# One of the sums of a Strassen-like product: a GpSimd addition, or a second activation and an adding transfer

## The chip, the cores and the metric

The kernel runs on one core of a Trainium2 chip. The metric is the device time of one execution in microseconds (us), lower is better. The kernel before took 1920.28 us (median of two runs, 1920.08 and 1920.47).

A core has engines that each work through their own instructions in order and wait for one another only through semaphores: TensorE (PE) multiplies matrices and leaves its results in PSUM, VectorE (DVE) and ScalarE (ACT) do elementwise work, GpSimd (POOL) does elementwise work on SBUF, and SyncE (SP) issues transfers here. Transfers run on 16 DMA engines; GpSimd, too, can issue them.

## The reference

Two parts, one behind the other. The first is the real part of a two-dimensional Fourier transform of each of 8 batches of 3008 x 256 numbers. The second is a small network on the 24064 rows that result: 256 to 2048 columns, the quick GELU, and back to 256.

```python
def _attn_ref(x):                       # x: (8, 3008, 256)
    X = np.fft.fft(x, axis=1)
    X = np.fft.fft(X, axis=2)
    return X.real.astype(np.float32)

def _moe_ref(x, w_in, w_out):           # x: (24064, 256)
    h = x @ w_in                        # w_in: (256, 2048)
    g = h * (1.0 / (1.0 + np.exp(-1.702 * h)))
    return (g @ w_out).astype(np.float32)
```

## The kernel before

All data are float32. The work is cut into steps: 8 batches, each with 3 blocks of 2 halves, each half with 8 pieces p of 256 hidden columns, so 384 steps in all. One step takes up to 256 columns of the transform (225 in one of the six halves).

In step t the kernel makes the hidden layer of step t and, with a lag of three steps, the product with w_out of step t-3. The hidden values of a step are four blocks of 128 partitions x n columns: h[:, half, f], with half for two mirrored frequencies and f for two groups of 128 hidden columns. They are called a11, a12, a21 and a22.

For the first 8 steps the product is done in the ordinary way. From step 8 on (t >= NP) it uses seven multiplications for a 2 x 2 block product in place of eight, in the manner of Strassen and Winograd. That needs four sums of the activated blocks for each step:

- s1 = a21 + a22 and s3 = a11 - a21, made by GpSimd;
- s2 = s1 - a11 and s4 = a12 - s2, made by VectorE.

```python
def hidden(t):                                   # TensorE, then ScalarE
    ...
    pa, pb = bank("pa"), bank("pb")              # PSUM, four banks in turn: two steps
    for ps, cs in ((pa, 0), (pb, 1)):
        for i in range(2):
            f = 2 * p + i
            nc.tensor.matmul(ps[:, i * 256:i * 256 + n], lhsT=wcs[cs][:, f * 128:(f + 1) * 128],
                             rhs=pq[:, cs, ks], start=True, stop=True)
    v = sp.tile([128, 512], F32, tag="v", name="v")
    nc.scalar.copy(two(v[:], n), two(pa[:], n))
    vb[t] = v, pa, pb

def rows(t):                                     # VectorE: the four blocks before the activation
    ...
    h = ht[t] = hp.tile([128, 2, 2, 256], F32, tag="h", name="h")     # four buffers
    dif = sp.tile([128, 512], F32, tag="dif", name="dif")
    nc.vector.tensor_tensor(two(h[:], n), two(v[:], n), two(pb[:], n), op=ALU.add)
    for i in range(2):
        ...
        nc.vector.scalar_tensor_tensor(dif[...], nb[:, ks], af2[:, f:f + 1], pb[...], op0=ALU.mult, op1=ALU.subtract)
    ...
            nc.vector.tensor_tensor(<second half of h, mirrored in runs of 32>, pa, dif, op=ALU.add)

def activate(t):                                 # ScalarE, in place
    b, blk, hh, p = steps[t]
    g = free(ht[t][:], 0, [256, 4], [1, width(blk, hh)])
    nc.scalar.activation(g, g, ACTF.Gelu_apprx_sigmoid)

def sums(t, eng):
    if not NP <= t < len(steps):
        return
    h, n = ht[t], width(*steps[t][1:3])
    a11, a12, a21, a22 = h[:, 0, 0, :n], h[:, 0, 1, :n], h[:, 1, 0, :n], h[:, 1, 1, :n]
    if eng is nc.gpsimd:
        st[t] = sp.tile([128, 4, 256], F32, tag="s", bufs=3, name="s")
    s1, s2, s3, s4 = (st[t][:, q, :n] for q in range(4))
    if eng is nc.gpsimd:
        eng.tensor_tensor(s1, a21, a22, op=ALU.add)
        eng.tensor_tensor(s3, a11, a21, op=ALU.subtract)
    else:
        eng.tensor_tensor(s2, s1, a11, op=ALU.subtract)
        eng.tensor_tensor(s4, a12, s2, op=ALU.subtract)

def product(t):                                  # TensorE, 14 matmuls; (bank, half, weights, data, ...)
    ...
        plan = ((0, 0, wo[:, p, 0, :], h[:, 0, 0, :n], 0), (0, 1, wt[:, p, 1, :], s[:, 1, :n], 0),
                (1, 0, wo[:, p, 2, :], h[:, 0, 1, :n], 0), (1, 1, wt[:, p, 2, :], s[:, 2, :n], 0),
                (2, 0, wt[:, p, 0, :], s[:, 0, :n], 0), (2, 1, wo[:, p, 3, :], s[:, 3, :n], 0),
                (3, 0, wt[:, p, 3, :], h[:, 1, 1, :n], 0))
    ...
```

The page counts each float32 matmul as two records, so the 4 matmuls of the hidden layer and the 7 of the product stand there as 8 and 14.

The order of a step in the program is the order in which each engine gets its work:

```python
for t in range(n + LAG):                         # LAG = 3
    if t < n:
        hidden(t)
    ...
    if t >= LAG:
        product(t - LAG)
    ...
    if 0 < t <= n:
        activate(t - 1)
        sums(t - 1, nc.gpsimd)
    sums(t - 2, nc.vector)
    if t < n:
        rows(t)
    if t >= LAG:
        combine(t - LAG)                         # VectorE, once in 8 steps: 7 operations, 2 transposes, stores
    for fn, args in extra.get(t, ()):            # the transform of the next batch, among the steps:
        fn(*args)                                # folds of x on GpSimd, small products, loads by SyncE
```

At the end there is no next step: the products of the last two steps are merged behind the third to last.

Of the kernel before, what the change touches and what calls it, by code (L numbers as in the profile page):

```python
# [27 lines left out]
F32 = mybir.dt.float32  # L28
U32 = mybir.dt.uint32
ALU = mybir.AluOpType  # L30
ACTF = mybir.ActivationFunctionType
# [15 lines left out]
def view(ap, offset, *dims):  # L47
    return bass.AP(ap.tensor, ap.offset + offset, [list(d) for d in dims])


def free(ap, offset, *dims):
    return bass.AP(ap.tensor, ap.offset + offset, [list(ap.ap[0])] + [list(d) for d in dims])
# [59 lines left out]
def kernel(ctx: ExitStack, tc, x, w_in, w_out, tab1, tab2, out):  # L112
    nc = tc.nc
# [12 lines left out]
    sp = ctx.enter_context(tc.tile_pool(name="sp", bufs=2, space=SB))  # L126
    op = ctx.enter_context(tc.tile_pool(name="op", bufs=2, space=SB))
# [330 lines left out]
    NP = NF // 2  # L458
    steps = [(b, blk, hh, p) for b in range(B) for blk in range(NBLK) for hh in range(2) for p in range(NP)]
    vb, ht, st, pot, ot = {}, {}, {}, {}, {}  # L460

    def width(blk, hh):

        return 225 if (blk, hh) == (0, 1) else 256
# [38 lines left out]

    def activate(t):
        b, blk, hh, p = steps[t]
        g = free(ht[t][:], 0, [256, 4], [1, width(blk, hh)])
        nc.scalar.activation(g, g, ACTF.Gelu_apprx_sigmoid)  # L507

    def sums(t, eng):

        if not NP <= t < len(steps):
            return
        h, n = ht[t], width(*steps[t][1:3])
        a11, a12, a21, a22 = h[:, 0, 0, :n], h[:, 0, 1, :n], h[:, 1, 0, :n], h[:, 1, 1, :n]
        if eng is nc.gpsimd:
            st[t] = sp.tile([128, 4, 256], F32, tag="s", bufs=3, name="s")
        s1, s2, s3, s4 = (st[t][:, q, :n] for q in range(4))
        if eng is nc.gpsimd:
            eng.tensor_tensor(s1, a21, a22, op=ALU.add)  # L519
            eng.tensor_tensor(s3, a11, a21, op=ALU.subtract)  # L520
        else:
            eng.tensor_tensor(s2, s1, a11, op=ALU.subtract)  # L522
            eng.tensor_tensor(s4, a12, s2, op=ALU.subtract)  # L523
# [115 lines left out]
    for e in odds:  # L639
# [7 lines left out]
                      in_=view(tab1, 0, [tab1.shape[1], 128], [28 * NM, 2], [1, ends]))  # L647
# [73 lines left out]
    n = len(steps)  # L721
# [38 lines left out]
    for t in range(n + LAG):  # L760
        if t < n:
            hidden(t)
        if t == 0:
            low_up(in2)
            nyquist(0, 0)
            low_down(in2)
        if t in rows_at:
            first_row(rows_at[t])
        if t >= LAG:
            product(t - LAG)  # L770
        if t in early:
            fold_w(early[t])
# [8 lines that stand above are left out]
            combine(t - LAG)  # L781
        for fn, args in extra.get(t, ()):
            fn(*args)
# [28 lines left out]
```

## Time and profile before

| | busy, us | share of the span | instructions |
|---|---|---|---|
| TensorE, matmuls | 1907.5 | 99% | 10720 |
| VectorE | 1415.3 | 74% | 2937 |
| GpSimd | 764.2 | 40% | 1057 |
| ScalarE | 675.0 | 35% | 932 |

| operation per step | line | engine | mean, ns | times |
|---|---|---|---|---|
| s1 = a21 + a22 | L519 | GpSimd | 720 | 376 |
| s3 = a11 - a21 | L520 | GpSimd | 735 | 376 |
| s2 = s1 - a11 | L522 | VectorE | 478 | 376 |
| s4 = a12 - s2 | L523 | VectorE | 528 | 376 |
| copy v <- pa | L482 | ScalarE | 578 | 384 |
| activation, in place | L507 | ScalarE | 1044 | 384 |

A row of the groups by line reads: line, engine, operation, what is written and what is read, the shape and the count; then the busy time in us and the mean in ns; then the engine's idle time just before these instructions and what ended most of it. The timeline gives the start in us from the span's start, the duration, the engine, the line, the operation and the count; in brackets stands the idle time before and its releaser. "PEld" is the loading of weights into TensorE, which runs beside the matmuls. The time in which an engine issues a transfer is not counted as busy.

The DMA queues moved 103.54 MB, nearly all from SyncE's queue; there is no transfer from GpSimd's queue.

### The profile page before, as it was taken

What the parts mean: (1) busy time and instruction counts of PE and PEld (TensorE: products, weight loads), DVE (VectorE), ACT (ScalarE), POOL (GpSimd) and SP (SyncE); (2) the same over time, 40 slices, a digit from 0 to 9 for tenths busy, and PEclk for the clock granted to TensorE, in tenths of its full rate; (3) what the DMA queues carried; (4) which work ended last, traced back from release to release, by engine and by line L of the source; (5) the groups of instructions that cost most, each with busy time, mean ns of one, the idle gap of its engine ahead of it and who ended that gap; (6) DMA issues with size and microseconds to landing.
All of it is one profiled execution on the core that took longest, in us unless ns stands there. A gap on an engine that the chain in (4) does not pass through costs nothing.

```text
span 1920.2 us, 29354 instructions
## 1 busy us (share of the span) xinstructions
PE 1907.5 (99%) x10720; PEld 1673.7 (87%) x10720; DVE 1415.3 (74%) x2937; ACT 675.0 (35%) x932; POOL 764.2 (40%) x1057
## 2 busy tenths in 40 slices
PE   8999999999999999999999999999999999999998
PEld 6798888988889888988889888898888988889887
DVE  7777677877787677777777777677777877778766
ACT  6533333333333333333333333333333333333332
POOL 4474224533256223552235523264323542223222
PEclk9999999999999999999999999999999999999999
DMA  8721530335212542226222172121820223202201
GB/s 269 174 51 35 113 36 12 59 57 102 17 23 48 90 69 24 51 28 105 40 28 50 43 107 32 16 49 43 124 19 12 17 50 54 17 12 27 17 12 23
DMA packets 145312, 103.54 MB, mean 54 GB/s; under 512 B 104914, under 2 KB 127986, under 8 KB 143984
## 3 DMA queue, kind: packets, MB, share of 16 engines
q1 hardware_dynamic: 143952, 101.14, 31.4%
q8 instruction: 85, 1.39, 0.3%
q10 hardware_dynamic: 1216, 0.52, 0.1%
q14 instruction: 59, 0.48, 0.1%
HBM read 58.38 MB, written 48.01 MB: 55 GB/s over the span
## 4 chain that ended last, share of the span: by engine, by line
PE 98%; DMA 1%; ACT 1%; DVE 0%; POOL 0%; SPq 0%; issue 0%; ACTq 0%; POOLq 0%
PE po L551 59%; PE pa L478 17%; PE pb L478 17%; PE ps L226 2%; PE ps L328 1%; PE ps L279 1%; DMA wo<-in_tab_dram 0%; DMA raw<-in_moe_w_out_dram 0%; PE psw L444 0%; ACT wo L251 0%; POOL wst L420 0%; PE psf L454 0%; ACT g L374 0%; ACT h L507 0%; DVE m L406 0%; DVE a L408 0%
## 5 line engine op out<-in xcount | busy, mean ns | idle before, releaser
L551 PE MATMUL po<-s,wo 128*128 128x256 f32 (+1 forms) x3008 | 758.4, 375 | 0.0
L519 POOL TENSOR_TENSOR s<-h 128x256 f32<-128x256 f32 (+1 forms) x376 | 270.8, 720 | 1085.0 <-ACT h L507 1020.6
L551 PE MATMUL po<-h,wo 128*128 128x256 f32 (+1 forms) x2384 | 689.3, 375 | 0.0
L551 PEld LDWEIGHTS po<-s,wo 128*128 128x128 f32 x3008 | 571.5, 190 | 64.5
L482 ACT COPY v<-pa 128x512 f32<-128x512 f32 (+1 forms) x384 | 222.1, 578 | 1061.9 <-PE pa L478 1061.9
L492 DVE TENSOR_TENSOR h<-v,pb 128x512 f32<-128x512 f32 (+1 forms) x384 | 259.0, 675 | 400.0 <-PE pb L478 386.6
L551 PEld LDWEIGHTS po<-h,wo 128*128 128x128 f32 x2384 | 452.8, 190 | 51.6
L507 ACT ACTIVATE h<-h 128x1024 f32<-128x1024 f32 (+1 forms) x384 | 400.9, 1044 | 17.9 <-DVE h L502 15.6
L478 PE MATMUL pa<-pq,wcs 128*128 128x256 f32 (+1 forms) x1536 | 393.9, 379 | 1.9 <-ACT h L507 1.7
L478 PE MATMUL pb<-pq,wcs 128*128 128x256 f32 (+1 forms) x1536 | 387.6, 375 | 0.0
L478 PEld LDWEIGHTS pa<-pq,wcs 128*128 128x128 f32 x1536 | 286.7, 190 | 50.5 <-issue 10.2
L495 DVE SCALAR_TENSOR_TENSOR dif<-nb,af,pb 128x256 f32<-128x256 f32 (+1 forms) x768 | 328.4, 469 | 0.9 <-ACT nb L346 0.9
L478 PEld LDWEIGHTS pb<-pq,wcs 128*128 128x128 f32 x1536 | 291.7, 190 | 33.2
L520 POOL TENSOR_TENSOR s<-h 128x256 f32<-128x256 f32 (+1 forms) x376 | 276.5, 735 | 0.0
L502 DVE TENSOR_TENSOR h<-pa,dif 128x512 f32<-128x512 f32 (+1 forms) x448 | 265.5, 605 | 13.2
L523 DVE TENSOR_TENSOR s<-h,s 128x256 f32<-128x256 f32 (+1 forms) x376 | 198.6, 528 | 12.9
L522 DVE TENSOR_TENSOR s<-s,h 128x256 f32<-128x256 f32 (+1 forms) x376 | 179.6, 478 | 4.3 <-POOL s L519 4.3
L199 POOL TENSOR_TENSOR xt<-xt 111x510 f32<-111x510 f32 x56 | 73.5, 1313 | 4.4
L585 DVE TENSOR_TENSOR c<-u,po 128x256 f32<-128x256 f32 (+1 forms) x188 | 69.5, 410 | 2.5 <-PE po L551 0.9
L334 DVE STREAM_TRANSPOSE pq<-ps 128x256 f32<-128x256 f32 x96 | 34.6, 418 | 44.9 <-PE ps L328 44.9
L585 DVE TENSOR_TENSOR u<-u,po 128x256 f32<-128x256 f32 (+1 forms) x141 | 57.8, 410 | 8.2 <-ACT u L556 2.5
L568 DVE STREAM_TRANSPOSE os<-c 128x512 f32<-128x512 f32 x93 | 60.4, 687 | 0.0
(73 smaller groups left out, 512.0 us busy)
## 6 DMA issues: line engine op xcount, KB each, us to landing
out_dram<-os SPq DMA_DIRECT2D x284, 64.0 KB
Td<-xt SPq DMA_DIRECT2D x14, 768.0 KB
t<-Td SPq DMA_DIRECT2D x7, 1536.0 KB
xt<-in_x_dram SPq DMA_DIRECT2D x14, 512.0 KB
xt<-Xr SPq DMA_DIRECT2D x14, 512.0 KB
nb<-pq SPq DMA_DIRECT2D x23, 256.0 KB
out_dram<-os SPq DMA_DIRECT2D x96, 56.0 KB
Xr<-in_x_dram SPq DMA_DIRECT2D x7, 752.0 KB
```

What stands on the lines that cost most here:

```text
L478: nc.tensor.matmul(ps[:, i * 256:i * 256 + n], lhsT=wcs[cs][:, f * 128:(f + 1) * 128], rhs=pq[:, cs, ks], start=True, stop=True)
L482: nc.scalar.copy(two(v[:], n), two(pa[:], n))
L492: nc.vector.tensor_tensor(two(h[:], n), two(v[:], n), two(pb[:], n), op=ALU.add)
L495: nc.vector.scalar_tensor_tensor(dif[:, i * 256:i * 256 + n], nb[:, ks], af2[:, f:f + 1], pb[:, i * 256:i * 256 + n], op0=ALU.mult, op1=AL ...
L502: nc.vector.tensor_tensor(free(h[:], 512 + at + m - 1, [256, 2], [RUN, blocks], [-1, m]), *ins, op=ALU.add)
L507: nc.scalar.activation(g, g, ACTF.Gelu_apprx_sigmoid)
L519: eng.tensor_tensor(s1, a21, a22, op=ALU.add)
L520: eng.tensor_tensor(s3, a11, a21, op=ALU.subtract)
L522: eng.tensor_tensor(s2, s1, a11, op=ALU.subtract)
L523: eng.tensor_tensor(s4, a12, s2, op=ALU.subtract)
L551: nc.tensor.matmul(pot[q][:, i, :n], lhsT=lhs, rhs=rhs, start=(p == 0 and i == 0 and f == 0), stop=(p == NP - 1), skip_group_check=True)
L585: nc.vector.tensor_tensor(out_, i0, i1, op=how)
```

## The change

The sum s1 = a21 + a22 is made in another way. ScalarE activates the raw block a22 a second time, straight into s1, before the in-place activation of all four blocks. Then a transfer from SBUF to SBUF, issued from GpSimd's queue, adds the activated a21 to it. GpSimd's addition of s1 falls away; s3 stays with GpSimd, s2 and s4 stay with VectorE. What is computed is the same. It is meant to take elementwise work off GpSimd, which shares the step with folds of the next batch's x, and give it to ScalarE and the DMA engines, which have more idle time. The buffer for the sums is taken one function earlier; there are still three of them.

```diff
     def activate(t):
         b, blk, hh, p = steps[t]
-        g = free(ht[t][:], 0, [256, 4], [1, width(blk, hh)])
+        n = width(blk, hh)
+        if t >= NP:
+            st[t] = sp.tile([128, 4, 256], F32, tag="s", bufs=3, name="s")
+            nc.scalar.activation(st[t][:, 0, :n], ht[t][:, 1, 1, :n], ACTF.Gelu_apprx_sigmoid)
+        g = free(ht[t][:], 0, [256, 4], [1, n])
         nc.scalar.activation(g, g, ACTF.Gelu_apprx_sigmoid)

     def sums(t, eng):
...
         a11, a12, a21, a22 = h[:, 0, 0, :n], h[:, 0, 1, :n], h[:, 1, 0, :n], h[:, 1, 1, :n]
-        if eng is nc.gpsimd:
-            st[t] = sp.tile([128, 4, 256], F32, tag="s", bufs=3, name="s")
         s1, s2, s3, s4 = (st[t][:, q, :n] for q in range(4))
         if eng is nc.gpsimd:
-            eng.tensor_tensor(s1, a21, a22, op=ALU.add)
+            eng.dma_start(out=s1, in_=a21, accum_op=ALU.add)
             eng.tensor_tensor(s3, a11, a21, op=ALU.subtract)
```

Lines of the changed kernel stand two to four lower than before: VectorE's s2 moves from L522 to L524, s4 from L523 to L525, and the in-place activation from L507 to L511.

## The prediction

> **What bounds the kernel now.** I read the page's first part (busy time of each engine), then the chain that ended last, then the groups by line, and last the timeline of two ordinary steps near the middle.
>
> ```profile
> PE 1907.5 (99%) x10720; PEld 1673.7 (87%) x10720; DVE 1415.3 (74%) x2937; ACT 675.0 (35%) x932; POOL 764.2 (40%) x1057
> PE 98%; DMA 1%; ACT 1%; DVE 0%; POOL 0%; SPq 0%; issue 0%; ACTq 0%; POOLq 0%
> L519 POOL TENSOR_TENSOR s<-h 128x256 f32<-128x256 f32 (+1 forms) x376 | 270.8, 720 | 1085.0 <-ACT h L507 1020.6
> L522 DVE TENSOR_TENSOR s<-s,h 128x256 f32<-128x256 f32 (+1 forms) x376 | 179.6, 478 | 4.3 <-POOL s L519 4.3
> ```
>
> TensorE is busy for 99% of the span and makes up 98% of the last chain. Its granted clock is 0.999 in the table of cores, and in the 10 us windows that I took from 600 to 1000 us it is busy for 10.00 of every 10.00 us. GpSimd, the engine that the change relieves, has 1085 us of idle time ahead of the very line that is removed. VectorE's next line waits for it only 4.3 us in the whole run.
>
> ```profile
> 1004.30 1.03 PE L478 MATMUL pa<-pq,wcs 128*128 128x256 f32 x4
> ...
> 1005.42 0.59 ACT L482 COPY v<-pa 128x512 f32<-128x512 f32 x1 [2.69 <-PE pa L478]
> ...
> 1005.90 1.06 ACT L507 ACTIVATE h<-h 128x1024 f32<-128x1024 f32 x1
> ...
> 1006.30 0.69 DVE L492 TENSOR_TENSOR h<-v,pb 128x512 f32<-128x512 f32 x1 [1.03 <-PE pb L478]
> ...
> 1007.10 0.73 POOL L519 TENSOR_TENSOR s<-h 128x256 f32<-128x256 f32 x1 [2.82 <-ACT h L507]
> ...
> 1007.80 0.69 DVE L502 TENSOR_TENSOR h<-pa,dif 128x512 f32<-128x512 f32 x1
> ...
> 1008.41 0.41 DVE L522 TENSOR_TENSOR s<-s,h 128x256 f32<-128x256 f32 x1
> ...
> 1008.86 0.42 DVE L523 TENSOR_TENSOR s<-h,s 128x256 f32<-128x256 f32 x1
> ...
> 1009.05 1.03 PE L478 MATMUL pa<-pq,wcs 128*128 128x256 f32 x4
> ```
>
> One step lasts 1009.05 - 1004.30 = 4.75 us; its 8 matmuls of the hidden layer and 14 of the product follow each other every 0.216 us. I set PE's start of step t at 0. The ScalarE copy of v(t) runs from 1.1 to 1.7. The activation of step t-1 comes behind it in ScalarE's order and ends at 2.7. GpSimd's s1(t-1) is there at 3.5. VectorE asks for it only at 4.1, after the three operations of rows(t). PE reads the finished sums of step t-1 in step t+2, after that step's hidden layer: at 9.5 + 1.7 + 0.4 = 11.6. So s1 has 0.6 us before VectorE stands still, and VectorE's sums have several us before PE does.
>
> **What the Trainium skill says.** "DMA: Bandwidth & Descriptors", section "Rules for kernel authors": accumulating during a transfer belongs on GpSimd's queue, the software descriptor path. So the engine that is relieved of an addition still writes descriptors. Its section "Anatomy of one DMA" gives a fit of about 2.0 us + bytes / 436 GB/s for one such transfer, most of the fixed part being the receipt of the last write; "Specifications" adds about 1 us to the first byte on this path. "Queues, rings and completion order" says that each DMA engine takes turns between queue rows by packets. The trace before has no transfer from GpSimd's queue, so it can neither confirm nor deny these figures. It does show that the DMA engines are busy: a share of 0.30 from 100 to 1900 us, and 0.93 to 1.08 from 660 to 690 us, while x is loaded.
>
> **The change, part by part.**
> 1. Removed: 376 additions on GpSimd, 270.8 us there. GpSimd falls from 764 to about 493 us of counted work, plus descriptor writing that the profile does not count as busy. None of it is on the path.
> 2. Added on ScalarE: 376 activations of 128x256. The copies and activations at L482 and L507 give the slope: (1060 - 586) ns for 512 more columns is 0.93 ns a column, so one costs about 0.35 us; the 128x256 copy at L556 takes 373 ns. That is 376 x 0.35 = 130 us, and ScalarE rises from 675 to about 805 us (42%). It stands in front of the large activation, so the end of that one moves from 2.7 to about 3.05.
> 3. Added: 376 transfers of 128 x 256 x 4 B = 128 KB. An estimate from the skill's figures: 2.0 + 0.3 for one pass of the bytes, 0.3 more because the sum is read as well as the addend, and 1.0 to write the descriptors: L = 3.6 us from GpSimd's start to landing. It could as well be 2.5 or 5; this is the number that I know least.
> 4. Moved: s1(t-1) is there at 3.05 + 0.15 (ScalarE's end to GpSimd's start, 0.13 in the trace) + L = 6.8 instead of 3.5. VectorE is free for it at 4.2 and waits 2.6 us. Before, it did the sums at once and then stood still for 1.75 us, from 5.0 to 6.75, where pb of the next step comes. So the new wait takes the place of the old one and is 0.9 us longer. The sums then end at 6.8 + 0.9 = 7.7 instead of 5.0, still 3.9 us before PE needs them at 11.6.
> 5. rows(t+1) starts at 7.7 instead of 6.75 and ends at 7.7 + 2.2 = 9.9. Its activation starts only behind v(t+2), at 9.5 + 1.6 = 11.1, in any case. So a delay of 1 us is still taken up there, and PE's step stays 4.75.
> 6. The end of the run has no next step to hide in. Before, the last activation ran from 1904.31 to 1905.37, s1 was there at 1906.2 and the first product that uses the last sums began near 1908.9. After, it is 1905.37 + 0.35 + 0.15 + 3.6 = 1909.5, and s2 0.4 later: PE waits about 1 us, once.
>
> **When it turns slow.** The parts of 4 and 5 form a ring over two steps: sums 0.87, rows 2.2, hand-over 0.1, the two activations 1.45, hand-over 0.15, then L. It closes in two steps, 9.5 us, while 4.75 + L <= 9.5, that is L <= 4.7 us. Where VectorE also has the combining of eight steps (seven operations of 0.41 and two transposes of 0.69, some 4.2 us once in 8 steps), part of the slack is gone, and I put the practical limit at 4.3 us. Beyond it, each 0.1 us of L costs 0.05 us a step, times 376 steps: 19 us. At L = 5.5 the ordinary step alone would be (4.75 + 5.5) / 2 = 5.13 us, and the run some 140 us longer.
>
> **Rivals.**
> - *Transfer hidden (my choice).* For it speak the idle time of GpSimd and VectorE and the 11.6 that PE waits for. The time is 1920 + 1 for the tail + some us of disturbed steps.
> - *Ring closes through the transfer.* The transfer takes over 4.3 us always, because descriptors are written slowly or the accumulating form is slow. The time would be 1960 to 2100. Against it stands only an estimate.
> - *Collision with the bulk loads only.* For some 40 us in each of the seven batches the DMA engines are full. There the transfer may take 5 to 6 us, so 8 steps would lose 0.15 to 0.6 us each, 1 to 5 us a batch, of which PE's slack of nearly 4 us takes up most. The whole would be 0 to 15 us.
> - *Faster.* PE has about 12 us that are not busy, at the start and the end, where the change does not act. GpSimd's lighter load frees VectorE from single delays (the longest L522 is 1482 ns against a median of 415), but VectorE was not the bound. I see nothing to gain.
>
> **Range and chances.** The middle case is 1920.3 + 1 (tail) + about 8 (disturbed and combining steps) = 1929 us. The lower end of 1918 is the present time less noise. The upper end of 2020 has the ring at L = 4.8. That L is beyond 4.3 to 4.5, where 2% (38 us) is lost, I give a third. Faster by over 2%: 0.01; within 2%: 0.65; slower by over 2%: 0.34.
>
> **What would show it.** ScalarE has 376 more activations of about 350 ns and a busy time near 805 us; GpSimd is near 493 us. L524 on VectorE (formerly L522) waits for the DMA in nearly every step, in total 376 x 2.6, about 950 us, and the 387 us of waiting at L492 for pb shrink to near zero. A distance of about 3.6 us from GpSimd's issue to the start of that line shows L. PE stays at 99% with steps of 4.75 us. I am wrong if PE has gaps at "po<-s" that wait for VectorE, or at pa for banks that rows has not given back; then L is over 4.3 us, or GpSimd is held so long by the descriptors that its folds of x (about 3.1 us in every other step of a stretch) push the next transfer back.

## The result, and the profile after

The changed kernel took 2217.82 us (median of 2216.15 and 2219.50) against 1920.28: ratio 1.1545, 95% interval 1.1523 to 1.1567. The prediction had 1929 and a range up to 2020; the run lies almost 200 us above that range.

The page after, first the busy time, then the two main DMA queues, then the engines' shares of the last chain:

```profile
PE 1995.3 (90%) x10720; PEld 1728.3 (78%) x10720; DVE 1431.3 (65%) x2937; ACT 834.7 (38%) x1308; POOL 844.6 (38%) x1057
...
q1 hardware_dynamic: 143952, 101.14, 27.2%
q0 software_dynamic: 54144, 48.29, 15.2%
...
PE 66%; DMA 21%; DVE 6%; issue 2%; ACT 2%; POOL 1%; DVEq 0%; SPq 0%; POOLq 0%; ACTq 0%
```

A fifth of the last chain (the chain of work that ended last, in which each piece waited for the one before) is now transfers. TensorE tells where the 297 us are: it stands for 2217.7 - 1995.3 = 222 us (before 13), and its busy time, for the same 10720 matmul records, has grown from 1907.5 to 1995.3. So some 210 us are new gaps, and 88 us are the same matmuls done more slowly; the mean granted clock is 0.945 after and 0.999 before.

Three lines of the groups say what the standing engines wait for:

```profile
L553 PE MATMUL po<-s,wo 128*128 128x256 f32 (+1 forms) x3008 | 801.3, 391 | 143.8 <-DVE s L524 143.8
...
L524 DVE TENSOR_TENSOR s<-s,h 128x256 f32<-128x256 f32 (+1 forms) x376 | 183.7, 489 | 669.6 <-DMA s<-h 635.4
...
L478 PE MATMUL pa<-pq,wcs 128*128 128x256 f32 (+1 forms) x1536 | 405.8, 388 | 65.8 <-DVE dif L495 63.8
```

VectorE's s2 waits for the adding transfer, TensorE's products wait for s2, and its hidden layer for PSUM banks that VectorE's rows, held up behind s2, have not read yet (143.8 and 63.8 us, nearly all of the 210). These are the two places where the prediction said that it would show itself wrong. The list of waits has the 635 us in 218 waits (total, number, longest):

```profile
DVE s L524 <- DMA s<-h: 635.4, 218, 13.6
```

A landing is the time from the issue of a transfer until its semaphore tells that it is done. The first line is the view of the tile s over the whole run, the second the same view from 750 to 790 us, while x is loaded, the third from 800 to 840 us, a quiet stretch. The windows behind them are of the same two stretches.

```profile
DMA to landing us min/median/max: 2.5/2.7/15.2
...
DMA to landing us min/median/max: 2.7/12.1/14.7
...
DMA to landing us min/median/max: 2.6/2.7/4.1
```

```profile
core 0: us, PE busy (x) PEld busy (x) DVE busy (x) ACT busy (x) POOL busy (x), PEclk, DMA share, GB/s
750.00:790.00 40.00, 24.66 (x96) 20.49 (x96) 14.06 (x31) 9.49 (x14) 7.80 (x10) 0.79 0.97 136
800.00:840.00 40.00, 40.00 (x246) 34.90 (x245) 29.79 (x64) 16.61 (x28) 13.58 (x17) 1.00 0.26 41
```

From 800 to 840 us the DMA engines are busy for a share of 0.26; the adding transfers land after 2.6 to 4.1 us there, and TensorE is busy for 40.00 of 40 us. From 750 to 790 us the share is 0.97, the median landing is 12.1 us, the longest 14.7, and TensorE stands for 15 us. Late landings are the exception: in the packet records 70 of the 376 transfers end over 5 us after their issue, mostly two in a row.

The loads of x are not the only such place. The timeline shows one stall with none of them near it. SyncE issues the broadcast of one row, nb<-pq, and the adding transfers come after it:

```profile
845.72 0.55 SPq L342 DMA_DIRECT2D nb<-pq  x1
...
846.60 1.06 ACT L511 ACTIVATE h<-h 128x1024 f32<-128x1024 f32 x1
...
848.19 0.87 POOL L521 DMA_DIRECT2D s<-h  x1 [4.97 <-ACT h L511]
...
848.80 1.03 POOL L522 TENSOR_TENSOR s<-h 128x256 f32<-128x256 f32 x1
...
851.08 0.87 POOL L521 DMA_DIRECT2D s<-h  x1 [1.26 <-PE po L553]
...
853.97 0.59 PE L553 MATMUL po<-h,wo 128*128 128x256 f32 x2
857.91 0.42 DVE L524 TENSOR_TENSOR s<-s,h 128x256 f32<-128x256 f32 x1 [8.95 <-DMA s<-h]
...
858.39 1.22 PE L553 MATMUL po<-s,wo 128*128 128x256 f32 x2 [3.83 <-DVE s L524]
```

```profile
847.00:856.00 9.00, 7.57 (x36) 6.31 (x34) 1.93 (x4) 3.21 (x5) 3.27 (x4) 1.00 0.89 28
856.00:858.00 2.00, 0.00 (x0) 0.00 (x0) 0.09 (x1) 0.00 (x0) 0.00 (x0) 0.72 0.89 131
858.00:863.00 5.00, 4.61 (x11) 3.71 (x12) 4.90 (x11) 1.47 (x2) 0.00 (x0) 0.50 0.01 2
864.00:867.00 3.00, 3.00 (x16) 2.64 (x15) 1.18 (x3) 1.96 (x3) 0.65 (x1) 1.00 0.32 49
```

The last three columns of the windows are the granted clock, the DMA share and GB/s. For 9 us the DMA engines are 0.89 busy and move only 28 GB/s. In the packet records of the trace these are packets of 2 KB that take 1.08 us each; other packets of 2 KB from the same queue have a median of 0.18 us. All 128 copies of the row are read from one partition. VectorE waits 8.95 us, TensorE 3.83. Then the clock is 0.50 for some 5 us, and a pair that took 0.59 us takes over 1 us. There are 23 such broadcasts. TensorE has 41 standstills of over 0.3 us from 90 us on, 208 us together; 26 of them, 127 us, begin within 13 us of the issue of a broadcast, some of these with loads of x close by.

The profile before has the same thing, and nobody waited for it there. This is its window from 734 to 740 us, in the broadcast issued at 730.69:

```profile
734.00:740.00 6.00, 6.00 (x29) 5.30 (x28) 3.42 (x8) 2.11 (x4) 1.42 (x2) 1.00 0.90 27
```

### The profile page after: what moved, and what is told of

It is laid out like the page before. It is cut to its first block, busy times and chain, and to the rows that moved or that the text cites. A ratio compares the mean times of both kernels' runs of the same rounds, so it can differ in the third digit from the quotient of the medians.

```text
span 2217.7 us, 30246 instructions
## 1 busy us (share of the span) xinstructions
PE 1995.3 (90%) x10720; PEld 1728.3 (78%) x10720; DVE 1431.3 (65%) x2937; ACT 834.7 (38%) x1308; POOL 844.6 (38%) x1057
## 4 chain that ended last, share of the span: by engine, by line
PE 66%; DMA 21%; DVE 6%; issue 2%; ACT 2%; POOL 1%; DVEq 0%; SPq 0%; POOLq 0%; ACTq 0%
PE po L553 41%; DMA s<-h 20%; PE pa L478 12%; PE pb L478 11%; DVE s L524 1%; DVE dif L495 1%; DVE h L492 1%; PE ps L226 1%; ACT h L511 1%; PE ps L328 1%; DVE h L502 1%; DMA raw<-in_moe_w_in_dram 1%; ACT s L509 0%; DVE c L587 0%; DMA raw<-in_moe_w_out_dram 0%
## 5 line engine op out<-in xcount | busy, mean ns | idle before, releaser
L553 PE MATMUL po<-s,wo 128*128 128x256 f32 (+1 forms) x3008 | 801.3, 391 | 143.8 <-DVE s L524 143.8
L521 POOL DMA_DIRECT2D s<-h x376 | 329.7, 877 | 1303.6 <-PE po L553 552.2
L553 PEld LDWEIGHTS po<-s,wo 128*128 128x128 f32 x3008 | 594.9, 199 | 228.2 <-DVE s L524 155.2
L553 PE MATMUL po<-h,wo 128*128 128x256 f32 (+1 forms) x2384 | 710.0, 384 | 0.3 <-DVE u L587 0.3
L524 DVE TENSOR_TENSOR s<-s,h 128x256 f32<-128x256 f32 (+1 forms) x376 | 183.7, 489 | 669.6 <-DMA s<-h 635.4
L553 PEld LDWEIGHTS po<-h,wo 128*128 128x128 f32 x2384 | 468.0, 196 | 58.5 <-DVE u L587 0.7
L478 PE MATMUL pa<-pq,wcs 128*128 128x256 f32 (+1 forms) x1536 | 405.8, 388 | 65.8 <-DVE dif L495 63.8
L511 ACT ACTIVATE h<-h 128x1024 f32<-128x1024 f32 (+1 forms) x384 | 399.6, 1041 | 11.9
L478 PE MATMUL pb<-pq,wcs 128*128 128x256 f32 (+1 forms) x1536 | 397.7, 382 | 1.4 <-DVE dif L495 1.4
L522 POOL TENSOR_TENSOR s<-h 128x256 f32<-128x256 f32 (+1 forms) x376 | 383.2, 1019 | 0.0
L492 DVE TENSOR_TENSOR h<-v,pb 128x512 f32<-128x512 f32 (+1 forms) x384 | 256.9, 669 | 43.9 <-PE pb L478 29.8
L509 ACT ACTIVATE s<-h 128x256 f32<-128x256 f32 (+1 forms) x376 | 156.1, 415 | 320.4 <-DVE h L502 315.3
L525 DVE TENSOR_TENSOR s<-h,s 128x256 f32<-128x256 f32 (+1 forms) x376 | 212.1, 564 | 12.9
```

What stands on the lines that cost most here:

```text
L509: nc.scalar.activation(st[t][:, 0, :n], ht[t][:, 1, 1, :n], ACTF.Gelu_apprx_sigmoid)
L521: eng.dma_start(out=s1, in_=a21, accum_op=ALU.add)
L553: nc.tensor.matmul(pot[q][:, i, :n], lhsT=lhs, rhs=rhs, start=(p == 0 and i == 0 and f == 0), stop=(p == NP - 1), skip_group_check=True)
```

## The experiments

My theory after this (A; the expectations call it A2 once the broadcasts are part of it): in each quiet step the transfer is hidden, as predicted. The loss comes where it stands behind other transfers that already hold the same 16 DMA engines, since VectorE works in order and holds up the next rows too. Rivals: the longer ScalarE work (B), GpSimd's time for the descriptors (C), the added traffic itself (D), the adding form, or the software queue. All times are medians; each ratio, with its 95% interval, is against runs of the kernel before on the same chip. The gains in us are against the 2217.82 of the changed kernel, which was not run again beside them; the medians of the kernel before lie between 1920.3 and 1922.1 us throughout.

**1. The activation without the transfer.**

```diff
-            eng.dma_start(out=s1, in_=a21, accum_op=ALU.add)
+            eng.tensor_tensor(s1, s1, a21, op=ALU.add)
```

> The second activation of a22 into s1 stays, but GpSimd adds a21 to it by an elementwise addition, without a transfer. Theory A (the transfer slows beside the bulk transfers and VectorE, in its order, stands still for it): no transfer, no loss, 1920 to 1923 us, TensorE 99% busy. Rival B (the longer work on ScalarE, 0.42 us a step ahead of the large activation, holds the ring): a good part of the 297 us stays, over 2000 us. Rival C (GpSimd's writing of descriptors): 1920 as well, so this run does not part A from C.

Measured: 1921.40 us, ratio 1.0003 (0.9994 to 1.0012). The second activation is there, 376 times:

```profile
L509 ACT ACTIVATE s<-h 128x256 f32<-128x256 f32 (+1 forms) x376 | 156.3, 416 | 15.7 <-DVE h L502 14.2
```

So 156 us of work on ScalarE cost nothing that can be measured. B falls.

**2. The transfer that nobody waits for.** Into the kernel before, beside its addition:

```diff
             eng.tensor_tensor(s1, a21, a22, op=ALU.add)
+            if t == NP:
+                pot["scr"] = cv.tile([128, 8, 256], F32, tag="raw", bufs=3, name="scr")
+                eng.memset(pot["scr"][:], 0.0)
+            eng.dma_start(out=pot["scr"][:, t % 8, :n], in_=wcs[0][:, 0:n], accum_op=ALU.add)
```

> The kernel before, with GpSimd's addition of s1 kept, and beside it in each step the same adding transfer within SBUF from GpSimd's queue, of a constant block into a scratch buffer that nothing reads. Theory A: the transfers land as late as in the changed kernel beside bulk transfers (up to 15 us), but nobody waits for them: 1920 to 1930 us. Rival C (what costs is GpSimd's time for writing descriptors, 0.88 us a step, and the slower s3 behind it): the loss or a large part of it appears here too, over 2000 us. Rival D (the 48 MB more traffic slows the loads of x so that the folds wait): over 1950 us, with waits of the folds for transfers.

Measured: 1925.43 us, ratio 1.0025 (1.0014 to 1.0035). The view of the scratch tile shows that the transfers were late as well:

```profile
DMA to landing us min/median/max: 2.5/2.7/14.5
```

The same traffic, the same descriptor work and the same late landings cost 4.5 us when nobody waits. C and D fall as causes of the 297; the loss needs somebody who waits.

**3. The loads of x left out** from the third batch on (so input is left out):

```diff
-            at(t0 + 10, turn, b + 2)
+            pass
...
-                at(t0 + 33 + late, load_x, b + 2)
+                pass
```

> The changed kernel without the loads of x and the copies of x within HBM from the third batch on (the folds work on what lies in the buffer, so this leaves out input). The spills and fills of the transform stay. Theory A: the stalls that stand in the loads of x and in those copies vanish in six of seven batches and those at spills and fills stay; by the idle time of TensorE per batch (some 30 us, about two thirds of it at loads of x and copies) I expect 2000 to 2060 us, and median landing unchanged at 2.7 us. If transfers were slow for a reason of their own (accumulating form, descriptors): still about 2200.

Measured: 2155.80 us, ratio 1.1223 (1.1204 to 1.1241). A miss: 62 us went, not 160 or more. I had counted TensorE's gaps by DMA share and had put most of them down to the loads. With these gone, most gaps that are left stand just behind nb<-pq, which comes some 85 us apart.

**4. VectorE's sums behind rows.**

```diff
-        sums(t - 2, nc.vector)
         if t < n:
             rows(t)
+        sums(t - 2, nc.vector)
```

> The changed kernel with VectorE's two sums of step t-2 behind rows(t) in place of ahead of it. The ring of waits then spans three steps: it closes without loss up to a landing of about 3 x 4.75 - 4.75 = 9.5 us, and TensorE's own need of the sums comes at a landing of 8 us. Theory A with the wait in VectorE's order as its lever: most of the loss goes, 1930 to 1990 us; the transfers over 8 us still stop TensorE. If it is the lateness for TensorE itself and not VectorE's order that costs: little changes, over 2150 us.

Measured: 2133.57 us, ratio 1.1109 (1.1093 to 1.1126). Also a miss, 84 us gained instead of over 200. What is left stands directly in front of the products, as in this line of its waits:

```profile
PE po L553 <- DVE s L524: 145.8, 47, 8.8
```

The later place helps the rows, but TensorE needs the sums at the same place in its order as before. By the 8 us of the expectation, a landing of 12 us is too late for that, however VectorE is ordered.

**5. The broadcasts by TensorE.**

```diff
-        if (b, blk) != (0, 0):
-            nc.sync.dma_start(out=nb[:], in_=free(row, 0, [0, 128], [1, 512]))
-            return
         ps = bank("psn")
         nc.tensor.matmul(ps[:], lhsT=ones[:], rhs=row, start=True, stop=True)
         nc.scalar.copy(nb[:], ps[:])
```

> The changed kernel with the 23 broadcasts of one row of 512 columns to all partitions (nb<-pq, 256 KB, all read from one partition) made by a matmul with ones and a ScalarE copy, as the first block already does, in place of a transfer. Theory A2 (each broadcast holds the DMA engines for some 10 us with packets of about 1.08 us, and the adding transfers stand behind it): some 5.5 us of TensorE's idle time and 2 us of slower clock per broadcast go, 23 x 7.5 = 170 us, less about 10 us for the new matmuls: 2030 to 2080 us. If only the large loads, spills and fills matter: 2200 to 2230 us.

Measured: 2079.15 us, ratio 1.0825 (1.0807 to 1.0843); and the control, the same edit in the kernel before:

> The kernel before with the broadcasts by TensorE, the control for what that costs by itself: 23 matmuls of 512 columns, about 0.43 us each, some 10 us, so 1925 to 1940 us.

1950.23 us, ratio 1.0151 (1.0136 to 1.0166). Its page:

```profile
PE 1934.8 (99%) x10766; PEld 1678.0 (86%) x10766; DVE 1413.1 (73%) x2937; ACT 689.3 (35%) x955; POOL 764.3 (39%) x1057
```

The control cost 29 us, not 10: 1.3 us for each broadcast, of which TensorE's busy time shows 27 (1934.8 against 1907.5). Against its control the changed kernel still loses 129 us of the 297; so 168 us go with the broadcasts, in line with the 170 expected.

**6. The large transfers spread.** The copy of x within HBM, the spill, the fill and the loads are cut and issued over several steps:

```diff
-            at(t0 + 10, turn, b + 2)
+            for i in range(8):
+                at(t0 + 10 + i, turn_part, b + 2, i)
...
-            at(t0 + 24 + late, spill, b + 1)
-            at(t0 + 29 + late, fill, b + 1)
+            for i in range(4):
+                at(t0 + 24 + i + late, spill_part, b + 1, i)
+                at(t0 + 29 + i + late, fill, b + 1, 3 * i, 3 * i + 3)
...
-                at(t0 + 33 + late, load_x, b + 2)
+                for i in range(8):
+                    at(t0 + 33 + 2 * i + late, load_x, b + 2, i)
```

> The changed kernel with the large transfers cut and spread over the steps: the copy of x within HBM in 8 parts over 8 steps, the spill in 4 and the fill in 4 parts over 4 steps each, the 8 loads of x one in every second step. The broadcasts stay. Theory A2: the stalls at the large transfers shrink and those at the broadcasts stay: 2110 to 2170 us. If the sum of bytes counted and not their bunching, or if only the broadcasts matter: 2200 us or more.

Measured: 2191.53 us, ratio 1.1405 (1.1381 to 1.1429). A miss, 26 us. The matmul records show where it stayed: TensorE's standstills that begin within 13 us of a broadcast's issue grew from 127 to 160 us, while all others fell from 81 to 32. In the timeline of this run parts of the loads now lie right beside a broadcast:

```profile
1100.18 0.63 SPq L192 DMA_DIRECT2D xt<-Xr  x1
1100.86 0.60 SPq L356 DMA_DIRECT2D nb<-pq  x1
1101.50 5.93 SPq L192 DMA_DIRECT2D xt<-in_x_dram  x1
...
1116.50 1.22 PE L567 MATMUL po<-s,wo 128*128 128x256 f32 x2 [7.21 <-DVE s L538]
```

**7. The three repairs together,** and then two at a time, all with the broadcasts by TensorE:

> All three together: broadcasts by TensorE, large transfers spread, VectorE's sums behind rows. Theory A2: nearly nothing is left to wait for, 1930 to 1960 us, landing of the adding transfers mostly 2.7 us, longest well under 10 us. If the transfer itself cost time in each step: over 2000 us.

> Broadcasts by TensorE and large transfers spread, VectorE's sums where the change has them. With the broadcasts gone (2079 us) the spreading no longer puts parts of the copy of x beside a broadcast, which is what I take to have spoilt the run with spreading alone. Theory A2: 2000 to 2050 us. If spreading has no worth by itself: 2070 us or more, and the gain down to 1981 us came from the later sums.

> Broadcasts by TensorE and VectorE's sums behind rows, large transfers unspread. Landings up to 12 us stay, and the ring over three steps closes up to 9.5 us, TensorE's own need up to 8. Theory A2: 2000 to 2040 us, with the stalls that are left in front of products that wait for the sums. If the order of VectorE gives nothing without spreading: 2070 us or more.

Measured: all three 1980.96 us (ratio 1.0309, 1.0294 to 1.0324); with spreading 2049.05 (1.0660, 1.0638 to 1.0682); with later sums 2010.27 (1.0461, 1.0445 to 1.0477). From 2079 spreading takes 30 us, later sums take 69, both 98. The first run lies above its range because the matmuls cost more than I had reckoned; it stands 31 us above its control. Why the later sums give more than spreading I did not separate.

**8. The form and the queue of the transfer.** A plain copy in place of the adding one, from GpSimd's queue and from ScalarE's (both leave a22 out of the sum):

```diff
-            eng.dma_start(out=s1, in_=a21, accum_op=ALU.add)
+            eng.dma_start(out=s1, in_=a21)
```

> The changed kernel with a plain copy of a21 into s1 in place of the adding transfer (a22 is left out of the sum), still from GpSimd's queue. Theory A2 (the wait behind other transfers costs, whatever this one does): 2150 to 2220 us, and landings up to about 15 us again. If the adding form is what is slow or what has to wait: under 2050 us.

```diff
+            nc.scalar.dma_start(out=s1, in_=a21)
```

> The same plain copy issued from ScalarE's queue, which builds its descriptors in hardware (a22 is left out of the sum). Theory A2 (all queues feed the same 16 engines and stand behind what these already hold): 2100 to 2230 us. If the software queue of GpSimd is what is served late: under 2000 us.

Measured: 2162.11 us (1.1257, 1.1235 to 1.1279) and 2108.00 us (1.0969, 1.0950 to 1.0987). The plain copy's queue and landing read:

```profile
q0 software_dynamic: 18048, 48.29, 6.5%
```

```profile
DMA to landing us min/median/max: 1.9/2.0/14.7
```

The plain copy from GpSimd's queue has a third of the packets (48 a transfer instead of 144) and lands 0.7 us sooner in the median, but as late at worst. The adding form is worth about 56 us of the 297, the software queue about 54 more; the greater part, 188 us, stays with a plain copy from a queue whose descriptors are made in hardware. From ScalarE's queue they are late as well: in the packet records 61 of the 376 end over 5 us after their issue, the latest 11.8 us. So waiting behind other transfers is no property of the adding form or of GpSimd's queue. The move to ScalarE's queue also puts the issue, 0.47 us a step, from GpSimd onto ScalarE, which I did not separate; and from that queue the plain copy, too, has 144 packets a transfer, so the 48 belong to the plain copy from GpSimd's queue and not to plain copies as such.

**9. The broadcast by way of HBM.** It was open what the broadcast holds without added matmuls, and whether any broadcast of 256 KB would do it:

```diff
-            nc.sync.dma_start(out=nb[:], in_=free(row, 0, [0, 128], [1, 512]))
+            at_ = (b * NBLK + blk) * 512
+            nc.sync.dma_start(out=view(Nd, at_, [512, 1], [1, 512]), in_=row)
+            nc.sync.dma_start(out=nb[:], in_=view(Nd, at_, [0, 128], [1, 512]))
```

> The changed kernel with each broadcast done in two transfers: the row of 2 KB to HBM, then from HBM to the 128 partitions. If reading one partition 128 times is what makes the packets take 1.08 us, the broadcast becomes short, nearly all of its 170 us go and no matmul is added: 2030 to 2070 us. If any broadcast of 256 KB holds the engines: over 2180 us.

> The control: the kernel before with the broadcast by way of HBM. Nobody waits for it there, so 1918 to 1924 us, and the DMA engines less busy.

Measured: 2073.67 us (1.0786, 1.0770 to 1.0802); the control 1921.76 us (0.9997, 0.9989 to 1.0006). This is the cleanest share: 144 us of the 297 go, by changing a transfer that the change did not touch, and in the kernel before the same edit is worth nothing. The window of the run in which the broadcast issued at 801.36 lies has a DMA share of 0.32, where the direct form filled 0.89; its packets of 2 KB take 0.08 us in the median there in place of 1.08:

```profile
801.00:806.00 5.00, 5.00 (x25) 4.41 (x24) 2.77 (x7) 2.96 (x4) 2.21 (x3) 1.00 0.32 79
```

So not any broadcast of 256 KB holds the engines; the one that reads a single partition of SBUF 128 times does.

**10. What is left without broadcasts.** Broadcasts by TensorE and no loads or copies of x from the third batch on (input is left out):

> The changed kernel with the broadcasts by TensorE and without the loads and copies of x from the third batch on (this leaves out input). Theory A2: of the 129 us that the run with broadcasts by TensorE alone stands over its control of 1950 us, the spills, fills and stores keep a third: 1980 to 2010 us. If loads of x cost nothing: 2070 us or more.

Measured: 2008.10 us (1.0448, 1.0428 to 1.0467), 71 us under the run of 5. The loads and copies of x account for a little over half of the 129 us that were left; 58 us stay beside spills, fills and stores.

**11. The version with all repairs,** the broadcast by way of HBM, spreading and later sums:

> Broadcast by way of HBM, large transfers spread, VectorE's sums behind rows. The same run with the broadcast by TensorE stood 31 us over its control. Theory A2: 1935 to 1960 us, the change nearly hidden at last. If the extra matmuls had hidden other costs: over 1980 us.

Measured: 1956.53 us, ratio 1.0181 (1.0164 to 1.0198):

```profile
PE 1917.7 (98%) x10720; PEld 1670.8 (85%) x10720; DVE 1586.8 (81%) x2937; ACT 826.0 (42%) x1308; POOL 844.9 (43%) x1057
```

Some 262 of the 297 us are back. The longest landing is 9.7 us. Of the 35 that are left, 10 are more busy time of TensorE and the rest are short gaps, mostly under 2 us; I did not trace them to single transfers. No version beats the kernel before, and with the same matmuls little could: TensorE stood for only 13 us there.

## Why the prediction was wrong, by its own steps

- **TensorE as the bound:** right for the kernel before. That taking the addition off GpSimd is worth nothing follows from TensorE's 99% there; no run took it away by itself. Experiment 1 has the ScalarE part alone at 1.0003.
- **Part 1, GpSimd at about 493 us:** wrong. It shows 844.6 us, more than the 764.2 before, so GpSimd was not relieved at all. Against what is said ahead of the prediction, the page counts the issue of these transfers as busy, at 877 ns each (329.7 us), and the record of s3 behind it overlaps with it and lasts 1019 ns in place of 735. Experiment 2 shows that this time is not on the path.
- **Part 2, 0.35 us an activation:** 0.415 us, so 156 us in place of 130. Harmless.
- **Part 3, L = 3.6 us:** the median is 2.7, below the estimate; without the 1.0 added for descriptors its sum would have been 2.6. In quiet stretches TensorE then stays busy as parts 4 and 5 have it: 40.00 of 40 us.
- **Part 4, a wait in nearly every step:** 218 of 376, in total 635 us against the 950 expected. That the total comes near is luck: from 800 to 840 us only 4 of 8 sums wait, 7.9 us together in place of 2.6 each, and the long waits lie in the stalls. The wait of L492 for pb did shrink, from 387 to 30 us.
- **Part 6, the tail:** TensorE waits 2.23 us in front of the last sums, about 1 expected, although the transfer was quicker than reckoned. TensorE was ready for them 1.6 us after the last activation and not 3.5, as in the kernel before.
- **"When it turns slow", the ring:** consistent with what the runs show. Moving the sums behind rows recovered 84 us, and 69 with the broadcasts gone. The limit of 4.3 us was not tried by itself. One term of it was too small: from the end of the activation to the issue it is mostly 0.53 us (846.60 + 1.06 to 848.19 above), 0.15 reckoned.
- **The step that failed is the third rival, the collision.** It was named, and given "5 to 6 us", 8 steps in each batch and 0 to 15 us in all. The landings were 12.1 and 13.4 us in the median in two stretches with loads of x, and 7.4 to 9.6 beside the broadcast shown, in place of 5 to 6; the loss was 297 us in place of 0 to 15. A landing of 12 us is over 8 us above the 3.6 reckoned, more than the slack of nearly 4 us could take up. And the rival had the collisions only in the loads of x: nearly half of the loss (144 us) lies at the 23 broadcasts. The 10 us windows on which the prediction rests already had one of them: from 730 to 740 us a share of 0.85 at 45 GB/s, beside 0.93 at 166 from 660 to 670.
- **A term that was missing:** the clock. 88 us of the 297 are slower matmuls. In the clock record of the run it drops to half 35 times while work goes on, each time after a standstill.

The Trainium skill's "DMA: Bandwidth & Descriptors", section "Queues, rings and completion order", says that a DMA engine alternates between queue rows by packets, and that such a packet is typically some 9 to 17 descriptors long. From the first half I took the small surcharge; the second is not in the prediction. In the packet records, adding transfers issued while a broadcast ran had their packets served only at its end (issued at 848.19, first packet at 855.88), and during the loads of x there are some 14 us without one: no interleaving that would have helped them. That need not contradict the page: by an estimate a broadcast gives each of the 16 engines only 8 of its 128 records, which may be one packet in the page's sense. No run shows where such packets end, or what the engines hold in advance.

## What to carry to other kernels

Judge a transfer that takes the place of a 0.7 us operation not by its landing in a quiet stretch but by its landing beside the busiest transfers of the kernel, against the time at which the bound engine needs the data. To find those, take DMA share and GB/s in windows of a few microseconds, and look for a high share at a low rate. A slow transfer for which nobody waits is free until something with a deadline shares its engines; here 23 broadcasts from one partition cost nothing before and 144 us after. When an in-order engine must wait for a transfer, place what others need from it ahead of the wait, and reckon the deadline of every reader, not only of the first.

## What the runs showed of the hardware that I had not expected

- A broadcast of a 2 KB row from one partition of SBUF to 128 holds all DMA engines for some 9 us at 27 to 28 GB/s, 1.08 us a packet of 2 KB. By way of HBM its packets took 0.08 us, and the share stayed at 0.32 over 5 us.
- The adding transfer of 128 x 1 KB from GpSimd's queue has 144 packets and a median landing of 2.7 us; the plain copy from the same queue 48 and 2.0 us; the plain copy from ScalarE's queue 144 again.
- After 2.3 us without a matmul (from 854.6 us) the granted clock fell to 0.50, and it came back 5.3 us after work had resumed. Over the run of the changed kernel the 35 drops came 2.0 to 5.4 us after a standstill began, and full clock 3.0 to 6.0 us after it ended; one standstill of some 3.4 us brought none.
- A broadcast by a matmul of one row with ones cost 1.3 us in the kernel before, where TensorE has no time to spare; the detour through HBM cost nothing there that could be measured.
